# A frequency-domain mixer and a two-layer block in one kernel: filter loads, a moved read, a changed step plan

## The chip, the cores and the metric

The kernel runs on one core of a Trainium2 chip. The metric is device time in microseconds, taken from the start to the end of one execution; the number shown is the median of three runs.

## What is computed

```
X = rfft(x, axis=1)                       # x: 8 batches x 3008 positions x 256 channels
Y = X * (filt_r + 1j * filt_i)            # one filter for all batches, 1505 frequencies x 256
y = irfft(Y, n=3008, axis=1)              # a circular convolution along the sequence
h = y.reshape(24064, 256) @ w_in          # 256 -> 2048
g = max(h, 0) + alpha * min(h, 0)         # one slope per hidden channel
out = g @ w_out                           # 2048 -> 256, float32
```

## The kernel before

The transform of length 3008 is split as 94 x 32 and done with matrix products in half precision. For each batch there are four kinds of pieces.

- `piece_a` (8 per batch): products with the 94-point table `wf1` (L152 to L157). ScalarE copies the result from PSUM into `asb`. `save_a` stores a quarter of `asb` to a scratch array `a_dram`; after all four, `turn_a` reads the array back in another order into `at`. This is "a batch's array": 1.57 MB, read by four loads, or by sixteen smaller ones for batches 1 and 2 (`quarters`).
- `piece_b` (6 per batch, L172): products of `at` with the table `twf`, into the PSUM tile `psF`; VectorE multiplies by the filter twice, into `ww` (with the swapped filter `filts_s`) and `uu` (with `filt_s`); four GpSimd DMAs then add `ww` onto `uu` with real and imaginary rows exchanged.
- `piece_c` (6, L192): products of `uu` with `twi` into a `psH` tile; ScalarE copies them to `v`. After every second one, `turn_c` stores eight rows to `v_dram`; the third `turn_c` then loads `zt` from there in four loads.
- `pair_d` (8, L235): the inverse 94-point products of `zt`, in `psF`; the result goes to `yT`, the input of the second part.

Batch 0 goes first and by itself, with its own forms of these pieces (`class First`): it has no GpSimd adds, and turns its arrays with products by an identity instead of DMAs. Its filter stands in `fst` in float32 (rows 0 to 8) and `filt_s` (rows 8 to 12, cast to half by GpSimd's DMA). `load_filt` issues eight DMAs per call, on SyncE or GpSimd. `behind` (L370) writes a few zeros into the part of `fst` that is to be loaded, so that SyncE's loads wait for VectorE to come to that place. After batch 0, `fst` is copied into `filt_s` (L405), and `filts_s` and the second half of the filter are made from it (L408, L410). `fst` and `asb` share one buffer.

Then come 48 blocks of 512 tokens (four of them 384) over 768 steps, 16 steps in a block. In a step, `up(j)` makes one 128-channel slice of `h` from `yT` in a `psH` tile; ScalarE copies each pair of slices to `gtb`, and VectorE makes `g` with three operations. In the same step `down` does a sixteenth of the previous block's products with `wout_s` (four of them, 256 columns wide, in a full block); when a group of token rows is through, ScalarE copies it to `osb` and SyncE stores it. After the last block its `down` remains alone.

The pieces of batches 1 to 7 are put into these steps by hand: `plan_fft(b, a_at, ta, quarters, x_at, b_at, c_at, d_at)` names the step of every piece (`ta` that of `turn_a`; `x_at` those of the loads of the next batch's x, four tiles). In a step that holds a `piece_a` or `piece_c` the down products go first (`front`). For batch b of 3 to 7 all steps are counted from p = 96 (b - 1), where `piece_b` begins at p + 2. The queues of all engines run in the order in which the code names the work; SyncE issues the scratch arrays' DMAs and the stores, GpSimd the loads with a cast and the adds.

Buffers: `psH` two PSUM tiles, `psO` two, `psF` one; `at`, `v`, `zt`, `asb` one each; `uu` three, `osb` three.

Of the kernel before, what the change touches and what calls it, by code (L numbers as in the profile page):

```python
# [9 lines left out]

FP16 = mybir.dt.float16
FP32 = mybir.dt.float32
# [5 lines left out]
D = 256  # L18
# [33 lines left out]
def kernel(  # L52
# [10 lines left out]
    nc = tc.nc  # L63
# [2 lines left out]
              for n, v in zip(names, _build_consts())}  # L66
    sgn = np.tile(np.repeat([1.0, -1.0], 32), 2)[:, None].astype(np.float32)
    sgn_d = nc.inline_tensor(sgn, name="c_sgn")
    id_d = nc.inline_tensor(np.eye(128, dtype=np.float16), name="c_id")

    konst = ctx.enter_context(tc.tile_pool(name="konst", bufs=1))
    p_x = ctx.enter_context(tc.tile_pool(name="p_x", bufs=4))
    p_fft = ctx.enter_context(tc.tile_pool(name="p_fft", bufs=1))
# [17 lines left out]
    filt_s = konst.tile([128, 12, 2, D], FP16, name="filt_s")  # L91
    filts_s = konst.tile([128, 12, 2, D], FP16, name="filts_s")
    al16 = konst.tile([16, 128], FP32, name="al16")
    id32 = konst.tile([16, 16], FP32, name="id32")
# [20 lines left out]
    def load_filt(eng, dst, ha, hb):  # L115
        n = hb - ha
        for i, src in enumerate((filt_r, filt_i)):
            for e in range(2):
                q = 64 * e + 32 * i
                k = 2 * ha + 24 * e  # L120
                for j, step, off in ((0, 1, k), (16, -1, N1 - k)):
                    eng.dma_start(
                        out=dst[q + j : q + j + 16, ha:hb].rearrange("p h r d -> p (h r) d"),
                        in_=bass.AP(tensor=src.tensor, offset=src.offset + off * D,
                                    ap=[[N1 * D, 16], [step * D, 2 * n], [1, D]]))
# [12 lines left out]
    class Fft:  # L138
        def __init__(self, b):
            self.b = b  # L140
            self.base = (b % 2) * NFFT
            self.uw = {}
# [29 lines left out]
        def piece_b(self, q):  # L172
            psf = banks(False)
            for h in range(2):
                for par in range(2):
                    r = slice(64 * par, 64 * par + 64)
                    for e in range(2):
                        k = 4 * q + 2 * h + e
                        nc.tensor.matmul(psf[64 * e : 64 * e + 64, par, 256 * h : 256 * h + 256],  # L179
                                         twf_s[r, k], self.at[r, k], start=True, stop=True)  # L180
            px = psf.rearrange("p r (h d) -> p r h d", h=2)
            uu = p_uw.tile([128, 2, 2, D], FP16, name="uu", bufs=3)
            ww = p_uw.tile([128, 2, 2, D], FP16, name="ww")
            fs, f = (t[:, 2 * q : 2 * q + 2].rearrange("p h r d -> p r h d") for t in (filts_s, filt_s))
            nc.vector.tensor_mul(ww, px, fs)  # L185
            nc.vector.tensor_mul(uu, px, f)  # L186
            for o in range(0, 128, 32):
                i = o ^ 32
                nc.gpsimd.dma_start(out=uu[o : o + 32], in_=ww[i : i + 32], accum_op=OP.add)  # L189
            self.uw[q] = uu  # L190
# [62 lines left out]
    class First(Fft):  # L253
        def __init__(self):
            super().__init__(0)
            self.at = p_fft.tile([128, NK, D], FP16, name="at")
            self.v = p_fft.tile([128, NK, D], FP16, name="v")
            self.zt = p_fft.tile([96, N2, D], FP16, name="zt")
            self.fst = p_fft.tile([128, 8, 2, D], FP32, name="fst", tag="asb")
            self.am = gtb[:, 0:6].rearrange("p a b c -> p (a b c)")  # L260
            self.vm = self.v.rearrange("p k d -> p (k d)")

# [19 lines left out]
        def piece_b(self, kp):  # L282
            hp = psH.tile([128, 2, 512], FP32, name="hps").rearrange("p r (i d) -> p r i d", i=2)
            for i in range(2):
                for par in range(2):
                    r = slice(64 * par, 64 * par + 64)
                    for o in (0, 32, 64, 96):
                        k = 2 * kp + o // 64
                        nc.tensor.matmul(hp[o : o + 32, par, i], twf_s[r, k, 32 * i : 32 * i + 32],
                                         self.at[r, k], start=True, stop=True, tile_position=(64 * par, o))  # L290
            uu = p_uw.tile([128, 2, 2, D], FP16, name="uu", bufs=3)
            fl = self.fst if kp < 8 else filt_s
            nc.vector.tensor_mul(uu, hp, fl[:, kp].unsqueeze(2).to_broadcast([128, 2, 2, D]))  # L293
            self.uw[kp] = uu

# [44 lines left out]
    def tables(eng, names, ka, kb):  # L340
        for n, t in (("twf", twf_s), ("twi", twi_s), ("twx", twx_s)):
            if n in names:
                eng.dma_start(out=t[:, ka:kb], in_=consts[n].ap()[:, ka:kb])

    xc = {(0, c): load_x(0, c) for c in range(4)}
    f0 = First()
    tables(nc.sync, ("twf",), 0, 8)
    load_filt(nc.sync, f0.fst, 0, 1)
    nc.sync.dma_start(out=al16, in_=moe_alpha.rearrange("(j p) -> j p", p=128))
    nc.sync.dma_start(out=sgn_s, in_=sgn_d.ap())  # L350
    nc.sync.dma_start(out=wf1_s, in_=consts["wf1"].ap())
    nc.sync.dma_start(out=wi3_s, in_=consts["wi3"].ap())
    load_filt(nc.gpsimd, filt_s, 8, 12)
    make_identity(nc, id32)
    for kt in range(2):
        nc.gpsimd.dma_start(out=win_s[:, kt], in_=moe_w_in[kt * 128 : (kt + 1) * 128])
    for q in range(2):
        nc.gpsimd.dma_start(
            out=wout_s[:, 8 * q : 8 * q + 8],
            in_=moe_w_out[1024 * q : 1024 * q + 1024].rearrange("(j p) d -> p j d", p=128))  # L360
# [6 lines left out]
            nc.tensor.matmul(pw[:, 0, 0:128], id16, id16, start=True, stop=True)  # L367

    warm(36)
    def behind(ha, hb):  # L370
        nc.vector.memset(f0.fst[:, ha:hb, :, 0:1], 0.0)
        load_filt(nc.sync, f0.fst, ha, hb)

    for i in range(8):
        f0.piece_a(i, both[i % 2], i % 3 < 2)
        if i % 2 == 1:
            warm((16, 8, 8, 8)[i // 2])
        if i == 3:
            behind(1, 4)
            tables(nc.sync, ("twi", "twx"), 0, 8)  # L380
        if i == 5:
            behind(4, 8)
            tables(nc.sync, ("twf", "twi", "twx"), 8, 24)
            alp = psO.tile([128, 2, D], FP32, name="op")
            nc.tensor.transpose(alp[:, 0, 0:16], al16, id32)
            nc.vector.tensor_copy(al_s, alp[:, 0, 0:16])
            nc.vector.tensor_scalar(alm_s, al_s, 1.0, -1.0, OP.mult, OP.add)
# [6 lines left out]
    for kp in range(0, 12, 2):  # L394
# [7 lines left out]
            f0.turn_at(kp + 6, 2, on_act)  # L402
        elif kp < 10:
            warm(4)
    nc.gpsimd.dma_start(out=filt_s[:, 0:8], in_=f0.fst)  # L405
    for o in range(0, 128, 64):
        for i in range(0, 64, 32):
            nc.gpsimd.dma_start(out=filts_s[o + i : o + i + 32], in_=filt_s[o + 32 : o + 64])  # L408
# [12 lines left out]
    for p in range(NB // 2):  # L421
        t = 0
# [19 lines left out]
    class Block:  # L442
# [25 lines left out]

        def start_down(self, last):
            n = self.tn // 128  # L470
            group = 1 if last else 2
            self.todo = []
            for s0 in range(0, n, group):
                s1 = min(s0 + group, n)
                for ka in (0, 8):
                    self.todo += [(s0, s1, si, k) for si in range(s0, s1) for k in range(ka, ka + 8)]

        def down(self, q):
            n = self.tn // 128
# [17 lines left out]
    def plan_fft(b, a_at, ta, quarters, x_at, b_at, c_at, d_at):  # L497
        f = Fft(b)
        for i in range(8):
            put(a_at[i], f.piece_a, i)  # L500
            front.add(a_at[i])
        for c in range(4):
            put(a_at[2 * c + 1], f.save_a, c)
            if b + 1 < NB:
                put(x_at[c],
                    lambda b=b, c=c: xc.update({(b + 1, c): load_x(b + 1, c)}))
        for q in range(quarters):
            w = NK // quarters
            put(ta, f.turn_a, nc.sync, w * q, w * q + w)
        for q in range(6):  # L510
            put(b_at[q], f.piece_b, q)
        for q in range(6):
            put(c_at[q], f.piece_c, q)
            front.add(c_at[q])
            if q % 2 == 1:
                put(c_at[q] + 1, f.turn_c, q // 2)
        for i in range(8):
            put(d_at[i], f.pair_d, i, on_act)
# [10 lines left out]
        put(19 + 2 * i, neg, 3 * i, 3 * i + 3)  # L529

    def d_steps(p):
        return [p + t for t in (88, 91, 104, 108, 116, 120, 140, 152)]

    plan_fft(1, (8, 12, 16, 18, 20, 22, 24, 26), 28, 4, (14, 20, 24, 28), (36, 44, 50, 56, 62, 68), (50, 56, 62, 68, 74, 80),
             (88, 91, 98, 101, 110, 118, 140, 152))
    plan_fft(2, (32, 38, 46, 54, 62, 68, 76, 84), 86, 4, (40, 56, 70, 86), (104, 114, 126, 136, 148, 158),
             (114, 126, 136, 148, 158, 170), d_steps(96))
    for b in range(3, NB):
        p = 96 * (b - 1)
        a_at = [p - 96 + t for t in (6, 10, 18, 22, 30, 34, 42, 46)]  # L540
        if b == 3:
            a_at = [t + 6 for t in a_at]
        plan_fft(b, a_at, p - 32, 1, [a_at[2 * c + 1] + 2 for c in range(4)],
                 range(p + 2, p + 74, 12), range(p + 14, p + 86, 12), d_steps(p))

    prev = None
# [48 lines left out]
```

## Time and profile before

| | us |
|---|---|
| median of three runs | 824.87 (822.88 to 827.63) |
| profiled execution | 825.72 |
| its span | 823.9 |
| TensorE busy | 776.5 |
| ScalarE busy | 583.1 |
| VectorE busy | 576.2 |
| GpSimd busy | 179.7 |
| mean granted TensorE clock | 0.974 |

The span runs from the first to the last instruction of the core. The rows of the profile give start and duration of (groups of) instructions, the engine (PE TensorE, PEld its weight loads, DVE VectorE, ACT ScalarE, POOL GpSimd, SPq SyncE's DMA queue), the line, output and input tiles, and in square brackets the idle time before, with what ended it. q0 is the queue of DMAs issued by GpSimd, q1 that of SyncE's.

### The profile page before, as it was taken

Reading aid. Unit: us, or ns where it says so; the run is one execution under the profiler, and the core shown is the slowest. Engines: PE = TensorE matmul, PEld = TensorE weight load, DVE = VectorE, ACT = ScalarE, POOL = GpSimd, SP = SyncE. Lnnn points to the kernel's source line nnn. Section 1 sums busy time; section 2 is a strip of 40 time slices with the busy share of each in tenths; the row PEclk is TensorE's granted clock in tenths of the full one; section 3 lists DMA queues with packets and bytes.
Section 4 is the critical chain, followed back from the end, with each engine's and each line's share of the span. In section 5 each row is a group of like instructions: output and inputs, shape, how many; then the busy total and the mean of one; then the engine's idle time right before and its main releaser. Section 6 shows DMA issues by size and latency. Waiting matters only on the chain. (4 is left out here: it accounts for less than half of the span.)

```text
span 823.9 us, 16322 instructions
## 1 busy us (share of the span) xinstructions
PE 776.5 (94%) x6495; PEld 521.6 (63%) x6495; DVE 576.2 (70%) x1080; ACT 583.1 (71%) x668; POOL 179.7 (22%) x257
## 2 busy tenths in 40 slices
PE   6479999799989999899999999999999999999997
PEld 5356666466656666566666666666666666676665
DVE  2367796387757778578766777768775888766663
ACT  2268687488756887588776887678866777676763
POOL 6112253032311333023320333113120212100000
PEclk8599999899999999999999999999999999999999
DMA  9986787757784665947675576855476344521111
GB/s 183 224 185 146 169 145 159 182 98 155 134 148 112 117 136 120 191 83 144 145 125 147 102 146 122 171 115 104 104 123 160 55 75 91 114 79 33 40 40 52
DMA packets 97357, 102.51 MB, mean 124 GB/s; under 512 B 11248, under 2 KB 82304, under 8 KB 96896
## 3 DMA queue, kind: packets, MB, share of 16 engines
q1 hardware_dynamic: 81616, 72.08, 34.1%
q0 software_dynamic: 15664, 29.38, 25.9%
q8 instruction: 51, 0.84, 0.4%
q14 instruction: 26, 0.21, 0.1%
HBM read 55.28 MB, written 46.66 MB: 124 GB/s over the span
## 5 line engine op out<-in xcount | busy, mean ns | idle before, releaser
L461 ACT ACTIVATE gtb<-hps 128x1024 f16<-128x1024 f32 (+1 forms) x384 | 386.1, 1006 | 145.4 <-PE hps L452 144.3
L452 PE MATMUL hps<-yT,win_s 128*128 128x512 f16 (+1 forms) x1536 | 437.8, 377 | 4.4 <-ACT v L245 2.3
L483 PE MATMUL op<-wout_s,gtb 128*128 128x256 f16 x3008 | 439.4, 274 | 1.4 <-DVE gtb L466 1.4
L483 PEld LDWEIGHTS <-gtb 128*128 128x128 f16 x3008 | 295.4, 98 | 173.0 <-issue 4.9
L464 DVE TENSOR_SCALAR m<-gtb,alm_s 128x512 f16<-128x512 f16 (+1 forms) x768 | 233.1, 346 | 197.3 <-ACT gtb L461 196.3
L466 DVE TENSOR_TENSOR gtb<-gtb,m 128x2048 f16<-128x2048 f16 (+1 forms) x192 | 231.0, 1203 | 10.4 <-PE hps L452 0.5
L189 POOL DMA_DIRECT2D uu<-ww x168 | 134.1, 1197 | 436.5 <-DVE uu L186 210.9
L452 PEld LDWEIGHTS <-win_s 128*128 128x128 f16 x1536 | 143.7, 98 | 64.2 <-issue 18.6
L245 ACT ACTIVATE asb<-hps 96x1024 f16<-96x1024 f32 x56 | 57.1, 1019 | 11.5 <-PE hps L155 11.3
L245 ACT ACTIVATE v<-hps 128x1024 f16<-128x1024 f32 x42 | 43.0, 1024 | 25.5 <-PE hps L202 25.5
L488 ACT ACTIVATE osb<-op 128x512 f32<-128x512 f32 (+1 forms) x98 | 56.3, 575 | 6.4 <-PE op L483 4.1
L112 POOL DMA_DIRECT2D xs<-in_x_dram x64 | 42.0, 781 | 68.6 <-PE hps L155 49.1
L245 ACT ACTIVATE yT<-psF 128x752 f16<-128x752 f32 x59 | 47.1, 797 | 13.7 <-PE psF L224 13.5
L185 DVE TENSOR_TENSOR ww<-psF,filts_s 128x1024 f16<-128x1024 f32 x42 | 51.1, 1217 | 0.0
L186 DVE TENSOR_TENSOR uu<-psF,filt_s 128x1024 f16<-128x1024 f32 x42 | 51.0, 1214 | 0.0
L224 PE MATMUL psF<-wi_s,zt 96*128 96x94 f16 x500 | 31.8, 208 | 7.1 <-DMA zt<-v_dram 6.5
L224 PEld LDWEIGHTS <-zt 96*128 96x128 f16 x512 | 29.2, 100 | 10.2 <-DMA zt<-v_dram 7.1
L155 PE MATMUL hps<-xs,wf_s 94*96 94x512 f16 x112 | 33.6, 381 | 0.0
L202 PE MATMUL hps<-uu,twi_s 64*64 64x256 f16 x336 | 18.2, 272 | 9.5 <-DMA uu<-ww 9.5
L293 DVE TENSOR_TENSOR uu<-hps,fst 128x1024 f16<-128x1024 f32 x8 | 9.5, 1221 | 13.2 <-DMA twi_s<-c_twi 10.8
L179 PE MATMUL psF<-at,twf_s 64*64 64x256 f16 x336 | 17.6, 281 | 0.4 <-DMA at<-a_dram 0.4
L245 ACT ACTIVATE v<-op 128x512 f16<-128x512 f32 x11 | 6.1, 595 | 16.0 <-PE op L308 16.0
(59 smaller groups left out, 151.6 us busy)
## 6 DMA issues: line engine op xcount, KB each, us to landing
out_dram<-osb SPq DMA_DIRECT2D x160, 128.0 KB
a_dram<-asb SPq DMA_DIRECT2D x28, 384.0 KB
uu<-ww POOLq DMA_DIRECT2D x168, 64.0 KB, 3.4
v_dram<-v SPq DMA_DIRECT2D x84, 128.0 KB
zt<-v_dram SPq DMA_DIRECT2D x28, 384.0 KB
at<-a_dram SPq DMA_DIRECT2D x20, 384.0 KB
xs<-in_x_dram POOLq DMA_DIRECT2D x32, 192.0 KB, 4.1
xs<-in_x_dram POOLq DMA_DIRECT2D x32, 184.0 KB, 5.3
```

The costliest lines, as they stand in the source:

```text
L112: nc.gpsimd.dma_start(out=xs[r], in_=xrow(b, c)[r])
L185: nc.vector.tensor_mul(ww, px, fs)
L186: nc.vector.tensor_mul(uu, px, f)
L189: nc.gpsimd.dma_start(out=uu[o : o + 32], in_=ww[i : i + 32], accum_op=OP.add)
L224: nc.tensor.matmul(ps[:, m], self.zt[:, 8 * g + 4 * mh + m, dh * 128 : dh * 128 + 128], wi3_s, start=True, stop=True)
L245: nc.scalar.activation(o, i, AF.Copy)
L452: nc.tensor.matmul(self.hps[:, j % 2, 0:tn], win_s[:, kt, j * 128 : (j + 1) * 128], yT[:, kt, self.t0 : self.t0 + tn], start=(kt == 0), st ...
L461: nc.scalar.activation(g[:, 2 * i : 2 * i + 2], self.hps[:, :, 0:tn], AF.Copy)
L464: nc.vector.tensor_scalar(m[:, 2 * i + h], g[:, 2 * i + h], 0.0, a, OP.min, OP.mult)
L466: nc.vector.tensor_add(g, g, m)
L483: nc.tensor.matmul(self.op[:, si - s0], self.gts[k][:, 128 * si : 128 * si + 128], wout_s[:, k], start=(si == s0 and k == 0), stop=(si == ...
L488: nc.scalar.activation(osb[:, 0:m], self.op[:, 0:m], AF.Copy)
```

## The change

Five edits.

1. Filter rows 4 to 8 go to `filt_s` by GpSimd, ahead of rows 8 to 12, instead of to `fst` by SyncE; `fst` is half as large and only rows 0 to 4 are copied from it. SyncE issues the rest of the tables `twf`, `twi`, `twx` right behind their first part, after the fourth `piece_a` of batch 0.
2. The 16 x 16 identity for the slopes comes from memory instead of being made on GpSimd.
3. The last block's down products: groups of 2, 1 and 1 token rows (128 tokens each) instead of four of one, and in each group the first 12 of 16 slices of all its rows before the last 4. The other blocks keep theirs (8 and 8).
4. For batches 3 to 7 `turn_a` moves from p - 32 to p - 15; for batch 2 from step 86 to 90.
5. The first two `pair_d` of each of the batches 1 to 7 move from 88 and 91 to 91 and 93 (counted from the batch's p). Batch 2's `piece_a` 3 to 7 (counted from 0) and batch 3's `piece_a` get other steps; their saves and the loads of x go with them.

```diff
+    id32_d = nc.inline_tensor(np.eye(16, dtype=np.float32), name="c_id32")
...
-            self.fst = p_fft.tile([128, 8, 2, D], FP32, name="fst", tag="asb")
+            self.fst = p_fft.tile([128, 4, 2, D], FP32, name="fst", tag="asb")
...
-            fl = self.fst if kp < 8 else filt_s
+            fl = self.fst if kp < 4 else filt_s
...
     nc.sync.dma_start(out=al16, in_=moe_alpha.rearrange("(j p) -> j p", p=128))
+    nc.sync.dma_start(out=id32, in_=id32_d.ap())
...
+    load_filt(nc.gpsimd, filt_s, 4, 8)
     load_filt(nc.gpsimd, filt_s, 8, 12)
-    make_identity(nc, id32)
...
-    def behind(ha, hb):
-        nc.vector.memset(f0.fst[:, ha:hb, :, 0:1], 0.0)
-        load_filt(nc.sync, f0.fst, ha, hb)
-
     for i in range(8):
         f0.piece_a(i, both[i % 2], i % 3 < 2)
...
         if i == 3:
-            behind(1, 4)
+            nc.vector.memset(f0.fst[:, 1:4, :, 0:1], 0.0)
+            load_filt(nc.sync, f0.fst, 1, 4)
             tables(nc.sync, ("twi", "twx"), 0, 8)
+            tables(nc.sync, ("twf", "twi", "twx"), 8, 24)
         if i == 5:
-            behind(4, 8)
-            tables(nc.sync, ("twf", "twi", "twx"), 8, 24)
...
-    nc.gpsimd.dma_start(out=filt_s[:, 0:8], in_=f0.fst)
+    nc.gpsimd.dma_start(out=filt_s[:, 0:4], in_=f0.fst)
...
         def start_down(self, last):
             n = self.tn // 128
-            group = 1 if last else 2
+            ends = [2, 3, 4] if last else list(range(2, n, 2)) + [n]
+            half = 12 if last else 8
             self.todo = []
-            for s0 in range(0, n, group):
-                s1 = min(s0 + group, n)
-                for ka in (0, 8):
-                    self.todo += [(s0, s1, si, k) for si in range(s0, s1) for k in range(ka, ka + 8)]
+            for s0, s1 in zip([0] + ends, ends):
+                for ks in (range(half), range(half, 16)):
+                    self.todo += [(s0, s1, si, k) for si in range(s0, s1) for k in ks]
...
     def d_steps(p):
-        return [p + t for t in (88, 91, 104, 108, 116, 120, 140, 152)]
-
-    plan_fft(1, (8, 12, 16, 18, 20, 22, 24, 26), 28, 4, (14, 20, 24, 28), (36, 44, 50, 56, 62, 68), (50, 56, 62, 68, 74, 80),
-             (88, 91, 98, 101, 110, 118, 140, 152))
-    plan_fft(2, (32, 38, 46, 54, 62, 68, 76, 84), 86, 4, (40, 56, 70, 86), (104, 114, 126, 136, 148, 158),
+        return [p + t for t in (91, 93, 104, 108, 116, 120, 140, 152)]
+
+    plan_fft(1, (8, 12, 16, 18, 20, 22, 24, 26), 28, 4, (14, 20, 24, 28), (36, 44, 50, 56, 62, 68),
+             (50, 56, 62, 68, 74, 80), (91, 93, 98, 101, 110, 118, 140, 152))
+    plan_fft(2, (32, 38, 46, 52, 58, 64, 70, 78), 90, 4, (40, 54, 66, 80), (104, 114, 126, 136, 148, 158),
              (114, 126, 136, 148, 158, 170), d_steps(96))
     for b in range(3, NB):
         p = 96 * (b - 1)
-        a_at = [p - 96 + t for t in (6, 10, 18, 22, 30, 34, 42, 46)]
-        if b == 3:
-            a_at = [t + 6 for t in a_at]
-        plan_fft(b, a_at, p - 32, 1, [a_at[2 * c + 1] + 2 for c in range(4)],
+        a_at = (10, 14, 22, 26, 34, 36, 44, 46) if b == 3 else (6, 10, 18, 22, 30, 34, 42, 46)
+        a_at = [p - 96 + t for t in a_at]
+        plan_fft(b, a_at, p - 15, 1, [a_at[2 * c + 1] + 2 for c in range(4)],
                  range(p + 2, p + 74, 12), range(p + 14, p + 86, 12), d_steps(p))
```

More of the change, by code (lines that the diff above doesn't have):

```diff
@@ L8 @@
 from concourse._compat import with_exitstack
-from concourse.masks import make_identity
 FP16 = mybir.dt.float16
```

## The prediction

> **What bounds the kernel now.** I read the page first: engines and slices.
>
> ```profile
> span 823.9 us, 16322 instructions
> ...
> PE 776.5 (94%) x6495; PEld 521.6 (63%) x6495; DVE 576.2 (70%) x1080; ACT 583.1 (71%) x668; POOL 179.7 (22%) x257
> ...
> PE   6479999799989999899999999999999999999997
> ```
>
> TensorE is the bound nearly everywhere; it lacks work only at the start (slices of 20.6 us: 6, 4, 7) and in a few later slices. What can be won is its idle time, 47 us, and the half clock behind it. So the second view is who TensorE waited for (total, times, longest):
>
> ```profile
> PE hps L202 <- DMA uu<-ww: 9.5, 5, 3.2
> PE psF L224 <- DMA zt<-v_dram: 6.5, 2, 6.0
> PE hps L289 <- DMA twf_s<-c_twf: 6.1, 1, 6.1
> PE hps L289 <- DVE uu L293: 3.4, 1, 3.4
> ...
> PE hps L452 <- ACT v L245: 2.3, 4, 0.6
> ...
> PE op L385 <- POOL id masks.py:199: 1.5, 1, 1.5
> ```
>
> Those six rows hold 29.3 us, and the change touches each. Everything below is made against the profiled execution: 825.72 us, its span and 1.8 around it. The median shown, 824.87, is 0.85 lower.
>
> **The start.** Timelines of VectorE, SyncE and GpSimd:
>
> ```profile
> 24.17 2.36 DVE L293 TENSOR_TENSOR uu<-hps,fst 128x1024 f16<-128x1024 f32 x2 [3.90 <-DMA twi_s<-c_twi]
> ...
> 36.28 2.36 DVE L293 TENSOR_TENSOR uu<-hps,fst 128x1024 f16<-128x1024 f32 x2 [6.91 <-DMA twi_s<-c_twi]
> ...
> 41.75 4.82 DVE L293 TENSOR_TENSOR uu<-hps,filt_s 128x1024 f16<-128x1024 f32 x4 [0.20 <-DMA xs<-in_x_dram]
> ```
> ```profile
> 17.85 0.34 SPq L343 DMA_DIRECT2D twi_s<-c_twi  x1
> ...
> 18.77 1.99 SPq L122 DMA_DIRECT2D fst<-in_filt_r_dram  x4
> 22.62 5.22 SPq L122 DMA_DIRECT2D fst<-in_filt_i_dram  x4
> 28.15 0.34 SPq L343 DMA_DIRECT2D twf_s<-c_twf  x1
> ```
> ```profile
> 13.32 0.54 POOL L122 DMA_DIRECT2D filt_s<-in_filt_i_dram  x1 [0.24 <-DMA xs<-in_x_dram]
> ...
> 40.97 0.58 POOL L405 DMA_DIRECT2D filt_s<-fst  x1 [0.91 <-DVE uu L293]
> ```
>
> The filter products run on VectorE at 1.2 us each, from fst or filt_s alike (2.36 for two, 4.82 for four), so the new operand type costs nothing. Two holes stand among them (the releaser that they name, twi_s, is only a load that landed about then; a product reads fst and what TensorE made). The second is the forward table's rest, issued at 28.15 behind the eight loads of filter rows 4 to 8. Without those, the table goes out right behind the inverse tables, about 19, 9 us sooner. The rows themselves take the place on GpSimd that rows 8 to 12 have now (last issue 13.32), and by the page's landing time they are there near 20:
>
> ```profile
> filt_s<-in_filt_i_dram POOLq DMA_DIRECT2D x4, 64.0 KB, 7.0
> ```
>
> The first hole is the loads of rows 1 to 4, landed at 24.2. How the hardware queue q1 fared beside GpSimd's (DMA answers for 12 to 18 us and 18 to 24 us; packets, MB, share):
>
> ```profile
> q1 hardware_dynamic: 687, 0.58, 55.0%
> ```
> ```profile
> q1 hardware_dynamic: 302, 0.36, 22.0%
> ```
>
> While GpSimd's queue carried filter rows, q1 moved 0.58 MB in 6 us; once it carried win_s, 0.36 MB. In the new order filter rows hold that queue to the mid twenties, so rows 1 to 4 land between 20.5 (first pace kept) and 24.2 (as now); I take 22.3. From there: two more products and the first piece_c pair, 5.2 us, then eight products at 1.23 and 0.5 of gaps. VectorE ends at 22.3 + 15.5 = 37.8; now it ends at 41.75 + 4.82 = 46.6. That is 8.8; for table waits that may remain I take off 0.6: **-8.2** (bounds -5 and -11). The identity from memory instead of GpSimd (1.5 in the waits) moves work ahead of this hole only, so it has no term of its own; the memset dropped is 0.07 us of an idle VectorE.
>
> What is late next: on GpSimd win_s, wout_s, batch 1's x and the copy out of fst move behind eight more loads. The copy shrinks to half, its 40.97 issue stays near 41, and batch 1's first piece_a (now 59, then 51) needs it landed, near 50. Cover is 1 us; if it is gone, each us late costs one.
>
> [...]
>
> ```profile
> 24.00:36.00 12.00, 3.24 (x78) 2.29 (x85) 3.58 (x3) 2.02 (x3) 1.16 (x3) 0.50 1.29 218
> ```
>
> The engines are indeed full here (share 1.29). But TensorE waits for one item in a queue's order, not for the last byte. The opposite reading is the second rival.
>
> **Steps.** Batch 2's and 3's piece_a leave the steps where piece_b and piece_c stand too (62, 68, 136, 148): the four ACT v waits of 0.56 go, -2.3. In exchange three of batch 3's now share a step with a pair_d (110, 118, 140), which takes no psH buffer; 0 to 0.56 each, I take 0.2: **-1.7** together.
>
> **Batch 1's first pair_d.** TensorE, SyncE, and the table by stretches (last columns: clock, DMA share, GB/s):
>
> ```profile
> 151.55 0.81 PE L224 MATMUL psF<-wi_s,zt 96*128 96x94 f16 x8 [6.01 <-DMA zt<-v_dram]
> ```
> ```profile
> 144.88 2.29 SPq L219 DMA_DIRECT2D zt<-v_dram  x4
> ```
> ```profile
> 150.00:155.00 5.00, 3.45 (x20) 2.34 (x21) 0.00 (x0) 1.27 (x2) 0.00 (x0) 0.53 0.81 222
> 155.00:160.00 5.00, 5.00 (x38) 3.69 (x37) 1.52 (x5) 2.59 (x4) 0.00 (x0) 0.79 0.31 86
> ...
> 335.00:340.00 5.00, 3.27 (x18) 1.71 (x19) 0.76 (x3) 1.99 (x2) 0.00 (x0) 0.80 1.17 196
> 340.00:345.00 5.00, 5.00 (x34) 3.36 (x32) 2.31 (x5) 2.72 (x4) 0.00 (x0) 0.86 0.54 132
> ...
> 620.00:625.00 5.00, 5.00 (x35) 3.25 (x34) 2.37 (x5) 3.58 (x4) 0.00 (x0) 1.00 0.73 164
> ```
>
> Step 88 becomes 91: three steps at 0.87 us (the pace is quoted below), less the piece_a that leaves the stretch, 2.2 us of cover. Batch 3's last x load and batch 2's last save move ahead of the v_dram writes, which takes them out of zt's way but into v's; I count 1.5 us for it. Wait left: 6.0 - 2.2 - 1.5 = 2.3, a gain of 3.7. The half clock after it cost (0.47 + 0.21) x 5 = 3.4, of which 0.8 fell into the wait: 2.6, and I keep 0.8 of that. **-5.5** (bounds -2 and -8.6).
>
> **The read moved by 17 steps.** Now, the last filter product's accumulating DMA and the 1.5 MB read of at run together, and piece_c waits:
>
> ```profile
> 336.73 0.41 PE L202 MATMUL hps<-uu,twi_s 64*64 64x256 f16 x6 [2.50 <-DMA uu<-ww]
> ```
>
> Moved behind that piece_c and turn_c, the read cannot delay it: the whole 9.5 goes, with the half clock behind two of the five waits, by the rows (0.20 + 0.14) x 5 = 1.7 each: **-12.9**. [...]
>
> ```profile
> 619.35 0.41 PE L202 MATMUL hps<-uu,twi_s 64*64 64x256 f16 x6 [3.18 <-DMA uu<-ww]
> ```
>
> I go by the rows. A second zt wait (6.5 - 6.0) goes with the first pair_d's later step: **-0.5**.
>
> Its price is the time to its own reader. SyncE issues it behind zt, and only out stores queue behind it (three osb buffers, two stores per eight steps, cover it). Batch 7 has no such read and shows the clean order: its last piece_c, then zt's read (717 to 723). Beside it the pace of an at read that has the engines alone (524 to 527), the reader of the batch after 336.73, and one step at the end:
>
> ```profile
> 709.64 0.41 PE L202 MATMUL hps<-uu,twi_s 64*64 64x256 f16 x8
> ```
> ```profile
> 717.00:723.00 6.00, 6.00 (x54) 4.68 (x53) 4.39 (x11) 4.00 (x6) 0.00 (x0) 1.00 0.95 263
> ...
> 524.00:527.00 3.00, 3.00 (x26) 1.66 (x24) 1.24 (x4) 2.52 (x3) 0.00 (x0) 1.00 1.24 195
> ```
> ```profile
> 358.00 0.41 PE L179 MATMUL psF<-at,twf_s 64*64 64x256 f16 x8
> ```
> ```profile
> 808.22 0.60 PE L483 MATMUL op<-wout_s,gtb 128*128 128x256 f16 x4
> ...
> 809.09 0.60 PE L483 MATMUL op<-wout_s,gtb 128*128 128x256 f16 x4
> ```
>
> From the last piece_c: zt is through 13.4 us later (723), the read then takes 1.57 MB (128 x 24 x 256 halves) at 195 GB/s = 8.1: landed at 21.5. Its reader, 24 steps on, stands at 24 x 0.87 + 0.7 for two pair_d = 21.6; where a block of 384 tokens lies between, at 358.00 - 336.73 - 1.7 = 19.6. So it is late by about 0.5 in three batches (landing included) and 2.2 in two: **+6** over five (bounds 0 and +12, with half clock). Batch 2's moves by four steps and goes in quarters, of which the reader needs one: 0.
>
> The other batches' first two pair_d stand three and two steps later than now; their yT is read from step 96 on, three steps or 2.6 us behind the second, and the eviction takes 0.8:
>
> ```profile
> L245 ACT ACTIVATE yT<-psF 128x752 f16<-128x752 f32 x59 | 47.1, 797 | 13.7 <-PE psF L224 13.5
> ```
>
> So 0 there; a later eviction would cost its lateness in each of seven batches.
>
> **Last block.**
>
> ```profile
> 814.17 5.84 PE L483 MATMUL op<-wout_s,gtb 128*128 128x256 f16 x52 [1.44 <-DVE gtb L466]
> ```
>
> Its down products begin with 24 matmuls that don't need the last gate, instead of 12. Twelve more at 5.84 / 52 = 0.11 us stand in the wait of 1.44: **-1.3**. The last two groups keep their size, so the evictions and stores behind them stay.
>
> **Sum.** -8.2 - 1.7 - 5.5 - 12.9 - 0.5 - 1.3 + 6 = -24.1: the profiled 825.72 becomes 801.6, the median 800.8. I say **801**.
>
> **The rivals.** (1) Slower: the moved read lands far too late. Its price decides: without the +6 the gains are 30.1, so the kernel is slower by more than 0.5% (about 4 us; less can't be told from no change by this measurement) once each of five batches waits 5.1 us and loses 1.7 of clock. That is the read at 120 GB/s. For it: q1 made 0.58 MB in 6 us, 97 GB/s, beside GpSimd's queue at the start; at that pace the read takes 16.2, is late by about 9, and five times 10.7 gives 848. Against: GpSimd's queue carries nothing there. 8%. (2) The shared engines decide the start: the bytes ahead of batch 1's piece_a drain no sooner, and of 8.2 only 2 stay: 807. Against: table bytes are a small part. 17%. [...] (3) The read lands in time and the tables early: no +6, start -11: 792. For it: the margin is near zero in three batches. 22%. (4) The moved read does not free the accumulating DMAs, since stores share their engines as well: no -12.9, 814. Against: batch 7, without a read, has no such wait. 6%. The forecast, 47%.
>
> **How the numbers follow.** With each unknown at its good end the median is 788 (start -11, pair_d -8.6, read 0), at its bad end 814 (-5, -2, +12). The range 787 to 815 takes in these and cases 2 to 4; rival 1 and some tails, about 15%, stay out. Faster by over 0.5%: all but rival 1 and a part of 4, 0.89; within 0.5% 0.03; slower 0.08.
>
> **What would show it.** Right: no wait of batch 0's piece_b for twf_s over 1 us, and the filter products end near 38; the uu<-ww row gone from TensorE's waits; zt under 3 us; a new row of psF in the other batches' piece_b waiting for at, about 6 us in five places; the last wait for gtb under 0.3. Wrong: that new row above 25 us; waits of asb, xs or filts_s in the first 70 us; uu<-ww waits that stay.

## The result, and the profile after

The changed kernel takes 816.17 us (median of four, 813.96 to 818.03); the kernel before, on the same chip, 826.25. The ratio is 0.9881 (95% interval 0.9837 to 0.9925): faster by 1.2%, where 3% was forecast, and just outside the range (787 to 815). The profiled span went from 823.9 to 814.6.

The page and TensorE's waits of the changed kernel (total, times, longest); those of the kernel before stand in the prediction:

```profile
span 814.6 us, 16313 instructions
...
PE 774.5 (95%) x6495; PEld 518.8 (64%) x6495; DVE 576.3 (71%) x1079; ACT 583.1 (72%) x667; POOL 183.7 (23%) x263
```
```profile
PE psF L179 <- DMA at<-a_dram: 12.1, 6, 3.5
PE hps L289 <- DVE uu L293: 6.3, 3, 5.3
...
PE psF L224 <- DMA zt<-v_dram: 2.4, 1, 2.4
...
PE psF L224 <- DVE uu L186: 1.0, 2, 0.7
...
PE hps L202 <- DMA uu<-ww: 0.2, 1, 0.2
```

The rows that the change aimed at are gone or small: uu<-ww 9.5 to 0.2, zt 6.5 to 2.4, twf_s and the identity gone. One row has grown from 0.4 and is now the largest: piece_b (L179) waits for at, 12.1 us. Batch 0's products (L289) wait 6.3 for VectorE instead of 3.4, which belongs to the start. But waits alone don't give the sum. What does is a comparison step by step: when the first product of `up` starts in the same step of both traces. The difference grows where the change wins time and shrinks where it loses it.

```
step   before   after    ahead by   what lies between
   0     53.0    45.5      7.5      the start
  72    130.1   121.2      8.9      two waits for v (steps 62, 68) gone, +1.0; step 34, +0.4
  96    161.0   145.3     15.7      batch 1's first pair_d, with 0.4 of a moved piece_a, +6.9
 160    226.8   211.4     15.4      new steps of batch 3, -0.4
 176    245.3   225.7     19.5      batch 2's last piece_c, no wait for uu
 200    268.0   252.6     15.4      batch 3's first piece_b, a wait for at
 272    343.5   323.7     19.9      the same pair for batches 3 and 4
 296    363.9   350.4     13.5
 392    458.4   447.3     11.1      batch 5's first piece_b, behind a gain of 1.4
 488    550.7   544.9      5.7      batch 6's, behind a gain of 1.0
 584    646.8   638.8      8.0      batch 7's, behind a gain of 3.5
 760    804.3   796.3      8.0
 end    823.9   814.6      9.3      last block, +1.3
```

From step 160 on the moved read brings 14.4 us (no waits for uu) and costs 21.8 (waits for at): a loss of 7.4 from the edit that was to win most.

The five places, on TensorE's timeline of the changed kernel:

```profile
244.66 0.41 PE L179 MATMUL psF<-at,twf_s 64*64 64x256 f16 x6 [2.23 <-DMA at<-a_dram]
```
```profile
341.98 0.63 PE L179 MATMUL psF<-at,twf_s 64*64 64x256 f16 x6 [3.54 <-DMA at<-a_dram]
```
```profile
439.32 0.49 PE L179 MATMUL psF<-at,twf_s 64*64 64x256 f16 x6 [1.87 <-DMA at<-a_dram]
```
```profile
536.45 0.63 PE L179 MATMUL psF<-at,twf_s 64*64 64x256 f16 x6 [3.15 <-DMA at<-a_dram]
```
```profile
632.87 0.41 PE L179 MATMUL psF<-at,twf_s 64*64 64x256 f16 x6 [0.91 <-DMA at<-a_dram]
```

These make 11.7 us. The rest of the 21.8 is in the table by stretches, right behind the waits (the third number from the end is the granted clock, then DMA share and GB/s; where the clock is down it stands at 0.50, as from 245.1 to 248.2):

```profile
245.00:250.00 5.00, 5.00 (x25) 2.88 (x24) 3.48 (x5) 1.14 (x2) 2.01 (x4) 0.66 0.22 38
340.00:345.00 5.00, 3.02 (x14) 1.35 (x15) 2.34 (x2) 0.00 (x0) 0.00 (x0) 0.55 0.43 119
345.00:350.00 5.00, 4.98 (x26) 2.77 (x25) 2.48 (x6) 3.12 (x4) 3.14 (x4) 0.77 0.53 52
...
440.00:445.00 5.00, 5.00 (x27) 3.00 (x26) 3.59 (x5) 1.49 (x2) 2.27 (x4) 0.71 0.17 22
535.00:540.00 5.00, 3.55 (x17) 1.70 (x18) 2.36 (x2) 0.41 (x1) 0.00 (x0) 0.51 0.28 90
540.00:545.00 5.00, 4.98 (x32) 2.91 (x31) 2.46 (x5) 3.19 (x4) 3.14 (x4) 0.81 0.53 52
630.00:635.00 5.00, 4.09 (x34) 2.46 (x32) 4.05 (x7) 2.42 (x4) 0.00 (x0) 1.00 0.78 160
```

The clock missing from these rows is (0.34 + 0.45 + 0.23 + 0.29 + 0.49 + 0.19) x 5 = 10 us, of which some 1.4 fall into the waits themselves. So half clock cost nearly as much as the waits; behind the fifth, of 0.91, there is none.

Why the read came late, for batch 4 (SyncE's queue, TensorE's last piece_c and the reader, the two stretches of DMA):

```profile
324.14 2.03 SPq L219 DMA_DIRECT2D zt<-v_dram  x4
326.21 1.19 SPq L431 DMA_DIRECT2D out_dram<-osb  x2
327.45 6.45 SPq L168 DMA_DIRECT2D at<-a_dram  x4
```
```profile
318.55 0.41 PE L202 MATMUL hps<-uu,twi_s 64*64 64x256 f16 x8
```
```profile
338.15 0.30 PE L179 MATMUL psF<-at,twf_s 64*64 64x256 f16 x2
```
```profile
325.00:331.00 6.00, 6.00 (x50) 4.62 (x48) 4.39 (x11) 3.70 (x5) 0.00 (x0) 1.00 0.95 243
333.00:339.00 6.00, 5.45 (x47) 3.81 (x45) 3.58 (x9) 4.91 (x7) 0.00 (x0) 1.00 1.25 181
```

The reader came 19.6 us behind the last piece_c, just as forecast. The array came after 23.4 instead of 21.5: two stores of 128 KB stood ahead of it (about 1 us, an estimate from the 243 GB/s), and its packets moved at 181 GB/s, not 195 (8.7 instead of 8.1 us). In the other four batches the array came 22.7 to 24.1 us behind the last piece_c.

### The profile page after: what moved, and what is told of

Same layout as the page of the kernel before. It is cut to its first block, busy times and chain, and to the rows that moved or that the text cites. A ratio compares the mean times of both kernels' runs of the same rounds, so it can differ in the third digit from the quotient of the medians.

```text
span 814.6 us, 16313 instructions
## 1 busy us (share of the span) xinstructions
PE 774.5 (95%) x6495; PEld 518.8 (64%) x6495; DVE 576.3 (71%) x1079; ACT 583.1 (72%) x667; POOL 183.7 (23%) x263
## 4 chain that ended last, share of the span: by engine, by line
PE 78%; DMA 11%; SPq 3%; ACT 3%; DVE 2%; issue 2%; POOL 1%; DVEq 0%; ACTq 0%; POOLq 0%
PE hps L449 35%; PE op L480 34%; DMA at<-a_dram 7%; SPq L168 3%; PE hps L155 2%; PE psF L224 2%; ACT gtb L458 2%; PE psF L179 2%; PE hps L202 1%; DMA xs<-in_x_dram 1%; DMA filt_s<-in_filt_i_dram 1%; DMA win_s<-in_moe_w_in_dram 1%; ACT asb L245 1%; DMA uu<-ww 1%; DVE uu L293 1%
## 5 line engine op out<-in xcount | busy, mean ns | idle before, releaser
L480 PE MATMUL op<-wout_s,gtb 128*128 128x256 f16 x3008 | 439.6, 274 | 0.1
L112 POOL DMA_DIRECT2D xs<-in_x_dram x64 | 39.7, 707 | 60.8 <-PE hps L155 49.5
L224 PE MATMUL psF<-wi_s,zt 96*128 96x94 f16 x500 | 31.2, 205 | 4.0 <-DMA zt<-v_dram 2.4
L224 PEld LDWEIGHTS <-zt 96*128 96x128 f16 x512 | 28.4, 98 | 7.4 <-DMA zt<-v_dram 2.7
L179 PE MATMUL psF<-at,twf_s 64*64 64x256 f16 x336 | 19.6, 287 | 12.2 <-DMA at<-a_dram 12.1
L179 PEld LDWEIGHTS <-twf_s 64*64 64x64 f16 x336 | 6.8, 105 | 22.1 <-DMA at<-a_dram 13.2
L155 PEld LDWEIGHTS <-wf_s 94*96 94x96 f16 x112 | 12.7, 125 | 0.9 <-issue 0.2
```

The source lines that it names most:

```text
L155: nc.tensor.matmul(ps[0:96, u], wf1_s, xs[:, o : o + 512], start=True, stop=True)
L224: nc.tensor.matmul(ps[:, m], self.zt[:, 8 * g + 4 * mh + m, dh * 128 : dh * 128 + 128], wi3_s, start=True, stop=True)
L480: nc.tensor.matmul(self.op[:, si - s0], self.gts[k][:, 128 * si : 128 * si + 128], wout_s[:, k], start=(si == s0 and k == 0), stop=(si == ...
```

## The experiments

Each is timed against the kernel before on the same chip (826.15 us on that of the first four, 825.21 on that of the others). The first three change the read alone, in the changed kernel, and the fourth fills the wait for it; the other four undo one part each in the best of these.

**The read in quarters.**

```diff
-        plan_fft(b, a_at, p - 15, 1, ...
+        plan_fft(b, a_at, p - 15, 4, ...
```

> The changed kernel, with the read at p - 15 split into four quarters of 12 rows for batches 3 to 7 (sixteen loads of 96 KB instead of four of 384 KB, same bytes, same place). The first piece_b needs one quarter only, the next stands 12 steps on. Theory 1 (the whole array lands too late): the first quarter lands some 6 us sooner than the whole, no wait for at: 794 to 797. Theory 2 (the place in the queue is the cost, or twelve more issues on SyncE hold the stores up): waits for at or for osb remain, 805 or more.

(The quarters are of 6 of the 24 rows; the text says 12.) Measured: 796.50 us, ratio 0.9613 (0.9555 to 0.9671). It beats both kernels. TensorE waits nowhere for at in batches 3 to 7 (the row of batch 4's reader has no idle time), SyncE takes 10.7 us to issue the sixteen loads, and from 30 to 790 us the granted clock is 1.00 (third number from the end):

```profile
322.96 10.68 SPq L168 DMA_DIRECT2D at<-a_dram  x16
```
```profile
333.56 0.41 PE L179 MATMUL psF<-at,twf_s 64*64 64x256 f16 x8
```
```profile
30.00:790.00 760.00, 745.83 (x6129) 499.35 (x6122) 562.76 (x1065) 572.02 (x654) 166.33 (x227) 1.00 0.59 126
```

The same bytes at the same place, in pieces that match what the reader needs first, win the whole 21.8 back in the traces: at the five places that lost time in the changed kernel (up to steps 200, 296, 392, 488 and 584) this run gains 4.15, 6.40, 3.79, 6.26 and 1.19 on it. By the medians it gains 19.7; elsewhere, up to step 176, the two run the same code, and their traces differ even so: this one's first block starts 2.7 us sooner (42.8 against 45.5), and it loses 2.0 between steps 104 and 160, where batch 2 waits for uu. Theory 1 is shown: the move was right, and what failed was waiting for the whole array.

**The read at its old place.**

```diff
-        plan_fft(b, a_at, p - 15, 1, ...
+        plan_fft(b, a_at, p - 32, 1, ...
```

> The changed kernel, with the read for batches 3 to 7 back at p - 32 and all else as changed: this one edit undone. Theory 1: the waits for at go (-21.9), those for uu<-ww come back with their half clock (9.0 + 3.4, by the offsets of the two traces 14.8): 809, between 806 and 812; the edit alone was a loss of 7. Theory 2: the same sum. A third, that the other edits lost time too and the read gained as forecast: 816 + 7 or more, 823.

Measured: 809.61 (807.10 to 815.98), ratio 0.9787 (0.9716 to 0.9858). The median is as theory 1 has it; the waits for uu are back (total, times, longest):

```profile
PE hps L202 <- DMA uu<-ww: 12.3, 6, 3.5
```

By the medians the rest of the change is thus worth more than the whole of it, and the moved read costs 6.6 us in this company. But the two intervals overlap, and the profiled execution, the slowest of the four, shows nearly nothing of it: its span is 814.1 against 814.6, since from step 160 on the waits for uu and half clock cost 20.6 us there, not 14.4. That the moved read was a loss is likely; its size is open.

**The read between the two.**

```diff
-        plan_fft(b, a_at, p - 15, 1, ...
+        plan_fft(b, a_at, p - 27, 1, ...
```

> The changed kernel, with the read of a batch's array for batches 3 to 7 at p - 27 instead of p - 15: five steps ahead of the last piece_c, seven behind the last piece_b. Theory 1 (the changed kernel lost 21.9 us because the whole array lands after its reader: 11.7 of waits and about 10.2 of half clock behind them, by its place behind zt's loads): the accumulating DMAs have landed by p - 27 and the read is through before the v_dram writes end, so neither the waits for at nor those for uu<-ww stand: 816.2 - 21.9 = 794, between 791 and 799. Theory 2 (the 1.57 MB collide with whatever runs beside them, and the collision only moves): the read now delays the v_dram writes and zt, pair_d waits for zt about 3 us in each of five batches with half clock behind some: 806 or more.

Measured: 812.86, ratio 0.9822 (0.9741 to 0.9903). Theory 1's number is missed. Theory 2's number (806 or more) holds, and so does its collision that only moves, but not its place: TensorE waits for zt once, as in the changed kernel, and for uu again.

```profile
PE hps L202 <- DMA uu<-ww: 10.7, 7, 3.4
```
```profile
306.35 0.41 PE L179 MATMUL psF<-at,twf_s 64*64 64x256 f16 x8
```
```profile
309.87 3.12 POOL L189 DMA_DIRECT2D uu<-ww  x4 [8.09 <-DVE uu L186]
```
```profile
311.79 4.48 SPq L168 DMA_DIRECT2D at<-a_dram  x4
```
```profile
320.57 0.44 PE L202 MATMUL hps<-uu,twi_s 64*64 64x256 f16 x6 [2.84 <-DMA uu<-ww]
```

What I had not counted stands in these rows: from piece_b to the first add it is 3.5 us, and GpSimd needs 3.1 more to issue all four. Seven steps behind piece_b the adds are only going out (309.9 to 313.0), and the read (from 311.8) falls on them. A place free of the adds and of the v_dram writes would have to lie behind the landing of the adds, and by then the writes are next; no run tries one.

**TensorE kept busy.** Products that nobody reads fill the wait.

```diff
+        if b > 2:
+            put(b_at[0], spin, 48)
...
+    def spin(n):
+        pw = banks(False)
+        for _ in range(n):
+            nc.tensor.matmul(pw[:, 0, 0:128], id16, id16, start=True, stop=True)
```

> The changed kernel, with 48 products of the identity with itself (128 columns, about 2.7 us at full clock, never read) put ahead of the first piece_b of each of batches 3 to 7, where TensorE waits for at. Theory 1 (the half clock behind the waits costs about as much as the waits): the five waits of 2.2, 3.5, 1.9, 3.2 and 0.9 become 2.7, 3.5, 2.7, 3.2 and 2.7 of work and rest, 14.8 instead of 11.7, and the 10.2 of half clock go: 816.2 - 7.1 = 809. The other reading (the waits alone cost, the clock rows are only a sign of them): 816.2 + 3.1 = 819.

(The 2.7 us of the fill are an estimate: a product of twice the width took 5.84 / 52 = 0.11 us in the kernel before, and 48 times half of that is 2.7. It took 2.84.) Measured: 811.61, ratio 0.9799 (0.9737 to 0.9860). Its stretches and the place of batch 4:

```profile
340.00:345.00 5.00, 4.98 (x36) 2.92 (x31) 4.72 (x7) 2.94 (x3) 1.91 (x4) 1.00 0.14 18
```
```profile
336.04 2.84 PE L497 MATMUL psF<-id 128*128 128x128 f16 x48
...
339.76 0.41 PE L179 MATMUL psF<-at,twf_s 64*64 64x256 f16 x6 [0.53 <-DMA at<-a_dram]
```

The array comes hardly sooner (339.8 against 342.0, in a trace that is 2.0 ahead), yet the clock stays at 1.00 and the five places together gain 6.3 us in the trace (7.1 expected, the times give 4.6); the fifth, whose wait was shorter than the fill, loses 1.6. The other reading, that clock rows are only a sign, would have cost 3. So half clock has a price of its own, and products of no use can save it.

**The start, and the order without the split.** Both put filter rows 4 to 8 back on SyncE and into `fst`, which is again for eight rows; the first ahead of the tables' rest, as in the kernel before, the second behind it.

```diff
-    load_filt(nc.gpsimd, filt_s, 4, 8)
...
-            tables(nc.sync, ("twf", "twi", "twx"), 8, 24)
         if i == 5:
+            nc.vector.memset(f0.fst[:, 4:8, :, 0:1], 0.0)
+            load_filt(nc.sync, f0.fst, 4, 8)
+            tables(nc.sync, ("twf", "twi", "twx"), 8, 24)
```

> The kernel with the read in quarters (796.5), with the old start: filter rows 4 to 8 by SyncE into fst, and the tables' rest behind them (the identity still from memory). Theory 1 (the start gave what the traces show between 7.5 and 10 us at the first block): 804 to 806. Theory 2 (the shared engines decide the start, what is won there is waited for at batch 1's x or asb): 799 or less.

```diff
-    load_filt(nc.gpsimd, filt_s, 4, 8)
...
             tables(nc.sync, ("twf", "twi", "twx"), 8, 24)
         if i == 5:
+            nc.vector.memset(f0.fst[:, 4:8, :, 0:1], 0.0)
+            load_filt(nc.sync, f0.fst, 4, 8)
```

> The kernel with the read in quarters (796.5), with filter rows 4 to 8 on SyncE as before, but behind the tables' rest instead of ahead of it: the order changed, the queue not split. Theory 1 (both the tables and the rows are wanted near 28 us, and what stands last in one queue comes last): the rows now land where the tables did, near 35, and the products wait for them: at most 2 us better than the old start, 802 to 806. Theory 2 (the split itself gives nothing, since all loads share the same engines; only the tables' place counted): 797, like the split.

Measured: 806.91, ratio 0.9770 (0.9718 to 0.9821), and 809.52, ratio 0.9812 (0.9766 to 0.9858). In the first the wait for the table is back:

```profile
PE hps L289 <- DMA twf_s<-c_twf: 6.6, 1, 6.6
```

By the times the start is worth about 10 us, a little over the 7.5 to 9.5 expected, but the size isn't firm. This run's first block starts at 57.7 us, 4.7 later than in the kernel before, though its start differs from that one only in where the identity comes from; the granted clock is 0.50 from 21 to 55 us here, and 0.67 on the mean from 12 to 53 us in the kernel before. The order alone wins nothing: it is no better than the old start. The table is there in time, and the products wait for the rows that now stand last, though SyncE had issued them all by 32.8:

```profile
41.44 4.84 DVE L293 TENSOR_TENSOR uu<-hps,fst 128x1024 f16<-128x1024 f32 x4 [11.08 <-DMA fst<-in_filt_i_dram]
```

**Later pair_d, and the new steps.**

```diff
-        return [p + t for t in (91, 93, 104, 108, 116, 120, 140, 152)]
+        return [p + t for t in (88, 91, 104, 108, 116, 120, 140, 152)]
```

> The kernel with the read in quarters (796.5), with the first two pair_d of every batch back at 88 and 91; all else kept. The offset between the traces of before and of the changed kernel grew by 8.4 us around batch 1's first pair_d, where 5.5 were forecast. Theory 1 (the later step gave about half, the batch 2 save and batch 3 load moved ahead of zt the rest): the wait for zt grows from 2.4 by three steps to about 5.0, with 3.4 to 6.8 us of half clock behind it, nothing in the other batches: 796.5 + 4 to 6 = 801 to 802. Theory 2 (the later step gave all of it): 805.

```diff
-    plan_fft(2, (32, 38, 46, 52, 58, 64, 70, 78), 90, 4, (40, 54, 66, 80), ...
+    plan_fft(2, (32, 38, 46, 54, 62, 68, 76, 84), 90, 4, (40, 56, 70, 86), ...
...
-        a_at = (10, 14, 22, 26, 34, 36, 44, 46) if b == 3 ...
+        a_at = (12, 16, 24, 28, 36, 40, 48, 52) if b == 3 ...
```

> The kernel with the read in quarters (796.5), with batch 2's and batch 3's piece_a, saves and loads of x at their old steps; pair_d stays at 91 and 93, batch 2's read at 90. Theory 1: the four waits of 0.56 for ACT's v come back (+2.3), those of pair_d for VectorE's uu (1.0) and some of 0.2 go, and zt of batch 1 lands some 3 us later behind the load of x (a wait of about 4 to 5 with half clock): 796.5 + 4 to 6 = 801 to 802. Theory 2 (as forecast, the steps gave 1.7 and zt's landing hangs on the pair_d step alone): 798.

Measured: 798.81, ratio 0.9678 (0.9631 to 0.9725), and 797.94, ratio 0.9656 (0.9604 to 0.9708). By the times neither differs clearly from 796.50; the intervals overlap, both come out below theory 1's 801, and the second is theory 2's 798. But the traces have theory 1's longer wait for zt:

```profile
139.68 0.76 PE L224 MATMUL psF<-wi_s,zt 96*128 96x94 f16 x8 [4.74 <-DMA zt<-v_dram]
```
```profile
141.82 0.81 PE L224 MATMUL psF<-wi_s,zt 96*128 96x94 f16 x8 [3.65 <-DMA zt<-v_dram]
```

The first is the earlier pair_d, the second the old steps; 2.38 with both edits in. Each brings half clock back: behind the wait the clock stands at 0.50 for 3.2 and 5.7 us (third number from the end):

```profile
139.90:143.10 3.20, 3.20 (x19) 2.09 (x18) 0.00 (x0) 1.29 (x2) 0.00 (x0) 0.50 0.93 275
```
```profile
141.90:147.60 5.70, 5.70 (x35) 3.96 (x36) 1.51 (x3) 2.82 (x4) 0.00 (x0) 0.50 0.61 199
```

At this place (steps 72 to 96) the two lose 4.0 and 4.7 us against the run in quarters, of which 1.6 and 2.9 are clock (half of these 3.2 and 5.7). So both edits carry part of that gain. Later steps give 2.4 and 1.4 of it back, in part because the run in quarters waits 1.4 us for uu at step 114 where these don't; so the times don't show it.

## Why the prediction was wrong

**The step that failed** is the price of the moved read, "+6 over five (bounds 0 and +12, with half clock)". It measured 21.8. Two things are wrong in it. The lateness was forecast at 0.5 and 2.2 us and was 0.9 to 2.2 and 3.2 to 3.5: in batch 4 the sum took the read at 195 GB/s where it made 181, and no store ahead of it. That made 11.7 of 5.9. The larger part is that the half clock was left out of the value, though the paragraph above it charges 1.7 us for it behind a wait of 2.50; its two waits of 2.2 would have asked for some 3 us even by the forecast lateness. Half clock came behind four of the five waits and made the other 10. The upper bound, +12, held some half clock and was too low as well. (The good end of the range adds up to 789, not 788; nothing hangs on it.)

The other steps, forecast against the traces: start 8.2, measured 7.5 (10 by the times of the run that undoes it; the forecast has no term for the half clock of the start, and a part of this may be that); steps 1.7, measured 0.6, since pair_d now waits for VectorE to free `psF` (the row L224 <- uu, 1.0); batch 1's pair_d 5.5, measured 6.9 (6.4 without the moved piece_a), with the wait as forecast (2.3, measured 2.4) but no half clock behind it; the adds 12.9 and 0.5, measured 14.4; last block 1.3, measured 1.3:

```profile
802.81 7.88 PE L480 MATMUL op<-wout_s,gtb 128*128 128x256 f16 x68
```

The last products now run through without a gap. All terms but one thus add up to 30.7 against 30.1. That they agree so well is partly luck: two came out 0.7 and 1.1 lower, two 1.4 and 1.0 higher.

In the start one step was wrong and made little difference: the products of rows 1 to 3 began not between 20.5 and 24.2 but at 25.4 (of what the row names as the last awaited, a table, they read nothing). SyncE's queue moved 0.46 MB from 12 to 18 us (0.58 before):

```profile
25.37 3.71 DVE L293 TENSOR_TENSOR uu<-hps,fst 128x1024 f16<-128x1024 f32 x3 [5.30 <-DMA twf_s<-c_twf]
29.84 6.88 DVE L293 TENSOR_TENSOR uu<-hps,filt_s 128x1024 f16<-128x1024 f32 x6 [0.76 <-DMA win_s<-in_moe_w_in_dram]
```

From there the products run almost without a hole, as the step said they would, and end at 39.6 (37.8 forecast, 46.6 before).

**The rivals.** The first, the read far too late, had the right mechanism with two fifths of its size; the point from which it decides, 6.8 us per batch with the clock, was not reached (4.4 on the mean). The second, that shared engines decide the start and only 2 us of it stay, is refuted: undoing the split cost 10 us by the times. The 2 us were an estimate that no run shows. The DMA engines were full in the kernel before (share 1.29 from 24 to 36 us, of it 0.71 by SyncE's queue and 0.57 by GpSimd's), and the split still won. Issue time is not excluded as a part of what it won: SyncE was at the eight loads from 18.8 to 27.8 us in the kernel before, and no run separates that from the order in the queue. The third needed the read in time, which it was only in quarters. The fourth is refuted by the 0.2 left of uu<-ww.

## What to carry to other kernels

A transfer that is moved out of one reader's way must be timed against its own reader from the issue of what stands ahead of it in the queue; where the margin is near zero, split it so that the first piece suffices, which won some 2.5% here (816.17 to 796.50 us). A wait of TensorE is to be priced at up to twice its length: the four of 1.87 to 3.54 cost 3.8 to 6.4 here, though others of 2.42 and 3.18 brought no half clock. To move a load back in its own queue won nothing here, where it is wanted as soon as what passes it (809.52 us against 806.91); on a second queue it won some 10 us (796.50).

## What was not expected of the hardware

- A wait of 1.87 us brought 3.4 us of half clock (below 1.00 from 439.5 to 442.9, 0.50 from 439.6 to 442.8), waits of 3.54 and 3.15 brought 6.8 (the clock missing from two rows, 0.68 x 5 / 0.5); others of 2.42 (at 140.8; 1.00 from 138 to 150) and 0.91 (1.00 from 630 to 635) brought none. In the kernel before, a wait of 2.50 (at 336.7) brought 0.80 and 0.86 in the two rows from 335 to 345, and one of 3.18 (at 619.4) left 1.00 from 615 to 625. Length alone does not decide it.
- With filter loads on both queues, from 12 to 18 us of the changed kernel, the two moved 0.53 and 0.46 MB (rows below); in the kernel before 0.56 and 0.58. Why, no run here tells.
- The same start code brought the first block at 42.8 to 45.5 us in seven profiled runs, so a difference of 2 us at the start of two traces says nothing.

```profile
q0 software_dynamic: 581, 0.53, 69.6%
q1 hardware_dynamic: 625, 0.46, 56.1%
```
